# A cross-network kernel: later tail copies for the first group, and tail turns first in the last but one group

## The chip, the cores and the metric

The kernel runs on one NeuronCore of a Trainium2 chip. The metric is device time in microseconds of one execution; most executions of one kernel agree within 0.3%. The profile covers one execution, from its first to its last instruction ("span"); the device time is about 1.8 us longer than that span (498.29 against 496.5 us in the profiled run of the kernel before).

## The reference

Six layers of a "cross network" over 16384 rows of 416 features, in bf16:

```
x = x0                                   # x0: [16384, 416]
for l in range(6):
    proj = x @ ws[l] + bs[l]             # ws[l]: [416, 416]
    x = x0 * proj + x
return x
```

## The kernel before

Rows are handled in 8 groups of 2048. A group is held turned, with features on partitions: three tiles of 128 features ("tiles" t = 0, 1, 2) and a tail of 32 features. A group has four chunks of 512 rows, and the tails of its four chunks are stacked on the four partition quarters. So an output tile is 12 matmuls of full 128 rows, and four of 32 rows that add the tail. ScalarE adds the bias while it empties PSUM, VectorE multiplies by x0 and adds x.

"Turn" in this document means a DMA that transposes. Each group is turned on its way in and out. For the first group, chunks 0 and 1 are loaded plainly and turned by TensorE (quick to start); chunks 2 and 3 are turned by DMA. Before the change, this part of the setup read:

```python
load_nat(0, 0, 2); load_nat(0, 2, KK)      # plain rows of chunk 0   (on SP's queue)
load_wm(0, "sp")                           # weights of layer 0
load_nat(1, 0, KK)                         # plain rows of chunk 1
load_w3(0, "act")                          # four small weight loads, on ScalarE's queue
half = slice(2 * CH, GC)
add("sp", lambda h: h.dma_start_transpose(Tb[:, half], g0[half, D - P:D]), writes=["Tb"], lane="Tb", batch=0)
for t in range(NT):                        # turned tiles of chunks 2 and 3
    add("sp", lambda h, t=t: h.dma_start_transpose(
        x0s[0][:, t * GC + 2 * CH:(t + 1) * GC], g0[half, t * P:(t + 1) * P]), ...)
for j in (2, 3):                           # tail copies, on ScalarE's queue, wait for Tb
    q = slice(j * T32, (j + 1) * T32)
    add("act", lambda h, q=q, j=j: h.dma_start(x0s[0][q, XW:XW + CH], Tb[P - T32:P, j * CH:(j + 1) * CH]),
        reads=["Tb"], writes=[("x03q", 0, j)], ...)
load_wm(1, "sp"); load_w3(1, "sp"); load_group(1)    # load_group(1) turns into Tb again
... (cut)

def first_job():                           # recorded after all of the above
    transposed_chunk(0)                    # TensorE turns; ScalarE and VectorE copy out of PSUM
    ... (bias, cut)
    full(g, l, 0, ba, True, True, chunks=[0])
    transposed_chunk(1)
    full(g, l, 0, ba, True, True, chunks=[1])
    full(g, l, 1, bb, True, True, chunks=[0, 1])
    full(g, l, 0, ba, True, True, chunks=[2, 3])
    rows32(g, l, 0, ba, False)             # first 32-row matmuls
    ... (cut)
```

Every operation goes through `add`, which orders it by its declared tokens: a read waits for the last *recorded* write of its token.

```python
def add(self, eng, fn, reads=(), writes=(), lane=None, batch=None, ...):
    for t in reads:
        w = self.writer.get(t)             # the last recorded writer
        if w is not None:
            deps[id(w)] = (w, True)
    ... (cut)
```

A group goes out through one buffer, `ost`, all on SP's queue, in program order:

```python
def output(g):
    turn(0); turn(1)                       # 128 features each, wait for tile 0 and tile 1
    for j in range(NJ):                    # four turns of the 32-feature tail
        add("sp", ... dma_start_transpose(ost[...], x3s[s3][q, :]) ...)
    turn(2)
    ... one store of ost, 1664 KB (two for group 0), waits for all turns
```

The last group (number 7) is not turned by DMA; TensorE computes its last layer with rows on partitions, and five stores on SP's queue and one on ScalarE's write it. The last output tile before that belongs to group 6: 12 full matmuls, then the four 32-row ones, then two evacuations of 1024 columns.

## Time and profile before

| | before |
|---|---|
| device time, median of 3 | 498.93 us (498.19 to 499.05) |
| span of the profiled run | 496.5 us |
| TensorE busy | 476.4 us |
| TensorE idle in one piece at the head | 5.50 us |
| first 32-row matmuls | 17.9 us |
| store of group 6 issued | 484.17 us |
| that store to the end of the span | 12.3 us |

From the page of the kernel before: the span, TensorE's line of busy time (share of the span, number of instructions), and the chain of waits by engine.

```profile
span 496.5 us, 7997 instructions
...
PE 476.4 (96%) x3205; PEld 200.6 (40%) x3205; DVE 404.0 (81%) x705; ACT 340.8 (69%) x366; POOL 11.6 (2%) x37
...
PE 92%; DVE 2%; DMA 1%; ACT 1%; issue 1%; SPq 0%; ACTq 0%; DVEq 0%
```

TensorE is the limit nearly everywhere, so a gain has to come from the edges. The chain of waits in the first microseconds shows one of them (columns: start in us, duration in us, what the chain stood on; "ACTq" is ScalarE's sequencer issuing a DMA):

```profile
2.67 6.36 DMA Tb<-in_x_dram
...
9.05 0.62 ACTq L494
...
9.69 0.69 ACTq L494
...
10.43 0.61 ACT x L531
...
11.09 1.52 PE ps L418 x3
...
17.93 0.33 PE ps L430 x4
18.25 1.40 PE ps L418 x6
...
27.80 0.61 PE ps L430 x8
```

L494 are the two tail copies; they wait for the turn into `Tb`, issued at 2.67 us, and ScalarE does nothing else until they are issued. L531 are the copies out of PSUM that TensorE waits for. TensorE had turned chunk 0 by 5.3 us, so it sat idle from about 5.6 to 11.09. L430 at 17.93 are the first 32-row matmuls, useful to compare by: all later work hangs on them. (The timelines below give them a start 0.06 to 0.07 us earlier than the chains, 17.86 for 17.93; L430 at 27.80 are those of the second layer.)

The other edge is the end. SP's queue of the kernel before, in order of time (start, duration in us, engine, line, operation, how many):

```profile
468.90 4.50 SPq L597 DMA_TRANSPOSE ost<-x  x2
473.45 6.34 SPq L605 DMA_TRANSPOSE ost<-x  x4
479.83 1.93 SPq L597 DMA_TRANSPOSE ost<-x  x1
484.17 0.37 SPq L615 DMA_DIRECT2D out_dram<-ost  x1
484.58 7.29 SPq L788 DMA_DIRECT2D out_dram<-x  x5
```

Turns 0 and 1 of group 6, its four tail turns, turn 2, then the 1664 KB store (L615), and behind it the stores of the last group (L788). The first two turns waited for VectorE's results; the tail turns, whose data had been ready since 459.7 us, queued behind them. The busy time by stretch (window, its length, busy time of the five engines with instruction counts, granted TensorE clock, busy share of the DMA engines, GB/s) shows what the last 12 us are made of:

```profile
core 0: us, PE busy (x) PEld busy (x) DVE busy (x) ACT busy (x) POOL busy (x), PEclk, DMA share, GB/s
484.20:488.00 3.80, 1.03 (x6) 0.44 (x4) 2.68 (x8) 1.03 (x2) 0.00 (x0) 1.00 0.78 260
488.00:492.00 4.00, 0.00 (x0) 0.00 (x0) 0.00 (x0) 0.00 (x0) 0.00 (x0) 0.63 1.08 339
492.00:496.50 4.50, 0.00 (x0) 0.00 (x0) 0.00 (x0) 0.00 (x0) 0.00 (x0) 0.50 0.79 237
```

From 488 us no engine computes; the DMA engines stream at about 340 GB/s until the last few us.

### The profile page before, as it was taken

What the parts mean: (1) busy time and instruction counts of PE and PEld (TensorE: products, weight loads), DVE (VectorE), ACT (ScalarE), POOL (GpSimd) and SP (SyncE); (2) the same over time, 40 slices, a digit from 0 to 9 for tenths busy, and PEclk for the clock granted to TensorE, in tenths of its full rate; (3) what the DMA queues carried; (4) which work ended last, traced back from release to release, by engine and by line L of the source; (5) the groups of instructions that cost most, each with busy time, mean ns of one, the idle gap of its engine ahead of it and who ended that gap; (6) DMA issues with size and microseconds to landing.
All of it is one profiled execution on the core that took longest, in us unless ns stands there. A gap on an engine that the chain in (4) does not pass through costs nothing.

```text
span 496.5 us, 7997 instructions
## 1 busy us (share of the span) xinstructions
PE 476.4 (96%) x3205; PEld 200.6 (40%) x3205; DVE 404.0 (81%) x705; ACT 340.8 (69%) x366; POOL 11.6 (2%) x37
## 2 busy tenths in 40 slices
PE   4999999999999999999999999999999999999990
PEld 2434434444444444444444444444444444443450
DVE  0578888888888888888888888888888888888892
ACT  2557667677677776677677767766767767776780
POOL 1010400000000000000000000000000000000000
PEclk9999999999999999999999999999999999999997
DMA  9966973000001377449325944460000434316168
GB/s 191 207 137 148 162 166 79 1 0 1 2 0 34 62 206 150 62 85 245 75 39 105 257 56 77 111 228 0 2 1 0 76 64 137 69 27 182 28 113 275
DMA packets 132521, 47.91 MB, mean 97 GB/s; under 512 B 111930, under 2 KB 131588, under 8 KB 132484
## 3 DMA queue, kind: packets, MB, share of 16 engines
q1 hardware_dynamic: 132040, 47.12, 43.0%
q8 instruction: 25, 0.41, 0.3%
q10 hardware_dynamic: 444, 0.28, 0.3%
q14 instruction: 12, 0.10, 0.1%
HBM read 5.12 MB, written 13.63 MB: 38 GB/s over the span
## 4 chain that ended last, share of the span: by engine, by line
PE 92%; DVE 2%; DMA 1%; ACT 1%; issue 1%; SPq 0%; ACTq 0%; DVEq 0%
PE ps L418 74%; PE ps L430 8%; PE ps L443 6%; PE ps L448 2%; PE ps L748 1%; DMA Tb<-in_x_dram 1%; DVE x L391 1%; ACT tw L377 1%; DVE tw L386 1%; PE ps L723 0%; SPq L473 0%; ACTq L494 0%; PE ps L521 0%; PE ps L759 0%; ACT x L776 0%
## 5 line engine op out<-in xcount | busy, mean ns | idle before, releaser
L377 ACT ACTIVATE tw<-ps,bias 128x1024 bf16<-128x1024 f32 (+1 forms) x293 | 299.6, 1076 | 131.5 <-PE ps L430 108.4
L418 PE MATMUL ps<-x,wm 128*128 128x512 bf16 x1692 | 380.4, 380 | 5.9 <-ACT x L531 5.5
L418 PEld LDWEIGHTS ps<-x,wm 128*128 128x128 bf16 x1692 | 159.0, 98 | 220.6 <-issue 28.3
L386 DVE TENSOR_TENSOR tw<-tw,x 128x1024 bf16<-128x1024 bf16 (+1 forms) x283 | 193.2, 687 | 65.8 <-ACT tw L377 65.5
L391 DVE TENSOR_TENSOR x<-tw,x 128x1024 bf16<-128x1024 bf16 (+1 forms) x283 | 181.2, 681 | 0.0
L430 PE MATMUL ps<-x,w 32*128 32x512 bf16 x564 | 44.5, 380 | 0.8 <-DVE x L408 0.8
L443 PE MATMUL ps<-x,wm 128*32 128x512 bf16 x564 | 38.7, 380 | 0.0
L404 ACT ACTIVATE ts<-ps,bias 128x512 bf16<-128x512 f32 x47 | 28.8, 701 | 0.0
L430 PEld LDWEIGHTS ps<-x,w 32*128 32x128 bf16 x564 | 9.1, 92 | 34.1 <-issue 32.6
L443 PEld LDWEIGHTS ps<-x,wm 128*32 128x32 bf16 x564 | 13.8, 96 | 15.7 <-issue 2.9
L408 DVE TENSOR_TENSOR x<-ts,x 128x512 bf16<-128x512 bf16 x47 | 18.6, 418 | 0.0
L406 DVE TENSOR_TENSOR ts<-ts,x 128x512 bf16<-128x512 bf16 x47 | 18.6, 419 | 0.0
L448 PE MATMUL ps<-x,wbd 128*32 128x512 bf16 x188 | 18.3, 379 | 0.0
L534 DVE COPY x<-ps 128x512 bf16<-128x512 bf16 x2 | 0.8, 425 | 12.9 <-PE ps L526 12.9
L293 POOL COPY wbd<-w 32x32 bf16<-32x32 bf16 x24 | 9.5, 396 | 43.2 <-DMA w<-in_ws_dram 42.0
L748 PE MATMUL ps<-wm,x 128*128 128x416 bf16 x48 | 9.2, 341 | 0.0
L531 ACT ACTIVATE x<-ps 128x512 bf16<-128x512 bf16 x4 | 2.2, 594 | 10.1 <-issue 8.2
L776 ACT ACTIVATE x<-ps 128x416 bf16<-128x416 f32 x15 | 7.4, 525 | 1.2 <-PE ps L748 1.1
L448 PEld LDWEIGHTS ps<-x,wbd 128*32 128x32 bf16 x188 | 5.0, 97 | 5.1
L748 PEld LDWEIGHTS ps<-wm,x 128*128 128x128 bf16 x48 | 5.1, 115 | 3.9 <-issue 1.4
L778 DVE TENSOR_TENSOR x<-x,x 128x416 bf16<-128x416 bf16 x15 | 5.5, 371 | 0.5 <-ACT x L776 0.2
L783 DVE TENSOR_TENSOR x<-x,x 128x416 bf16<-128x416 bf16 x16 | 5.6, 368 | 0.0
(36 smaller groups left out, 35.3 us busy)
## 6 DMA issues: line engine op xcount, KB each, us to landing
out_dram<-ost SPq DMA_DIRECT2D x6, 1664.0 KB, 6.9
x<-in_x_dram SPq DMA_DIRECT2D x5, 416.0 KB, 7.5
wm<-in_ws_dram SPq DMA_DIRECT2D x6, 312.0 KB, 3.1
out_dram<-ost SPq DMA_DIRECT2D x2, 832.0 KB, 5.2
out_dram<-x SPq DMA_DIRECT2D x3, 416.0 KB, 7.3
x<-Tb SPq DMA_DIRECT2D x28, 32.0 KB, 1.8
ost<-x SPq DMA_TRANSPOSE x49, 3.4
w<-in_ws_dram SPq DMA_DIRECT2D x20, 26.0 KB, 2.2
```

The lines of the kernel that those rows point to most:

```text
L293: add("pool", lambda h, q=q: h.tensor_copy(wbd[l][q, q], w3[l][q, NT * P:D]), reads=[("w3", l, j)], writes=[("wbd", l)])
L377: add("act", lambda h, a=a, w=w, b0=b0: h.activation(tw[r][:, a * CH:(a + w) * CH], psum[:, b0 * CH:(b0 + w) * CH], ACT_F.Identity, bias=b ...
L386: add("dve", lambda h, a=a, e=e: h.tensor_tensor(tw[r][:, a * CH:e * CH], tw[r][:, a * CH:e * CH], x0s[s0][:, i * GC + a * CH:i * GC + e * ...
L391: add("dve", lambda h, a=a, e=e: h.tensor_tensor(xs[so][:, i * GC + a * CH:i * GC + e * CH], tw[r][:, a * CH:e * CH], src(i, a, e), ALU.ad ...
L404: add("act", lambda h: h.activation(ts[r][:, :], bank(b), ACT_F.Identity, bias=bias[:, 3, l:l + 1], scale=1.0), reads=[("ps", b), "bias"], ...
L406: add("dve", lambda h: h.tensor_tensor(ts[r][:, :], ts[r][:, :], x0s[s0][:, XW:XW + CH], ALU.mult), reads=[("ts", r)] + x03_toks(s0), writ ...
L408: add("dve", lambda h: h.tensor_tensor(x3s[so][:, :], ts[r][:, :], src, ALU.add), reads=[("ts", r)] + stok, writes=[("x3", so)], hold=True)
L418: add("pe", lambda h, t=t, j=j: h.matmul(bank(banks[j]), wm[l][:, t, ecols], src(t, j, j + 1), start=(first and t == 0), stop=(not first a ...
L430: add("pe", lambda h, q=q, j=j: h.matmul(bank(banks[j]), w3[l][q, ecols], src[q, :], start=first, stop=not first, tile_position=(j * T32, 0)),
L443: add("pe", lambda h, t=t, j=j, src=src, l=l, b=b: h.matmul(bank(b, j * T32, (j + 1) * T32), wm[l][:, t, NT * P:D], src(t, j, j + 1), star ...
L448: add("pe", lambda h, j=j, s3=s3, l=l, b=b: h.matmul(bank(b, j * T32, (j + 1) * T32), wbd[l][:, j * T32:(j + 1) * T32], s3, start=False, s ...
L748: add("pe", lambda h, t=t: h.matmul(bank(b, n=D), xcol(t, j, kk), wm[l][:, t, :], start=(first and t == 0), stop=(not first and t == NT - 1)),
```

## The change

Intent: (1) at the head, don't let ScalarE's queue stand on the turned tail; issue the tail copies behind the PSUM copies. For that the tail gets a buffer of its own (a work buffer not used yet), and the four small weight loads go to SP's queue. (2) At the end, let group 6 turn its tails first, and finish its last tile sooner: 32-row matmuls first, then the full ones chunk by chunk, each chunk evacuated on its own.

```diff
-    load_w3(0, "act")
+    load_w3(0, "sp")
@@
-    add("sp", lambda h: h.dma_start_transpose(Tb[:, half], g0[half, D - P:D]), writes=["Tb"], lane="Tb", batch=0)
+    add("sp", lambda h: h.dma_start_transpose(tw[NTW - 1][:, half], g0[half, D - P:D]),
+        writes=[("tw", NTW - 1, j) for j in (2, 3)], lane="Tb0", batch=0)
@@
-    for j in (2, 3):                      # tail copies, in the setup
-        q = slice(j * T32, (j + 1) * T32)
-        add("act", lambda h, q=q, j=j: h.dma_start(x0s[0][q, XW:XW + CH], Tb[P - T32:P, j * CH:(j + 1) * CH]), ...)
@@ first_job
         transposed_chunk(1)
+        for j in (2, 3):
+            q = slice(j * T32, (j + 1) * T32)
+            add("act", lambda h, q=q, j=j: h.dma_start(
+                x0s[0][q, XW:XW + CH], tw[NTW - 1][P - T32:P, j * CH:(j + 1) * CH]),
+                reads=[("tw", NTW - 1, j)], writes=[("x03q", 0, j)], lane="x03_00", batch=0)
@@ output
-        turn(0)
-        turn(1)
+        if g < LAST - 1:
+            turn(0)
+            turn(1)
         ... (four tail turns)
+        if g == LAST - 1:
+            turn(0)
+            turn(1)
         turn(2)
@@ order of matmuls in the last tile
+    mode[len(items) - 1] = "RF"
@@
             rows32(g, l, i, banks, True)
-            full(g, l, i, banks, False, False)
-            evacuate(g, l, i, banks, list(range(NJ)), 2)
+            if n == len(items) - 1:
+                full(g, l, i, banks, False, True, lambda j: evacuate(g, l, i, banks, [j], 1))
+            else:
+                full(g, l, i, banks, False, False)
+                evacuate(g, l, i, banks, list(range(NJ)), 2)
```

More of the change, by code (lines that the diff above doesn't have):

```diff
@@ L491, in bass_standalone__cross_network_dcn__recsys_kernel @@
             writes=[x0_tok(0, t, j) for j in (2, 3)], lane=f"x0_00{t}", batch=0)
-    for j in (2, 3):
-        q = slice(j * T32, (j + 1) * T32)
-        add("act", lambda h, q=q, j=j: h.dma_start(x0s[0][q, XW:XW + CH], Tb[P - T32:P, j * CH:(j + 1) * CH]),
-            reads=["Tb"], writes=[("x03q", 0, j)], lane="x03_00", batch=0)
     load_wm(1, "sp")
```

## The prediction

> **What bounds the kernel.** TensorE: busy 476.4 of 496.5 us (page, part 1), clock granted 0.993; the chain of waits is 92% TensorE. The change touches two stretches outside this middle.
>
> *Head.* The chain stands on a DMA: `Tb<-x0` is issued at 2.67 us and lands at 9.03. ScalarE's queue holds two tail copies that wait for it (9.05, 9.69) ahead of the PSUM copies, so ScalarE starts those at 10.43, although TensorE finished the transposes at 5.3. TensorE sits idle 5.50 us, till 11.09 (view of waits). The first 32-row matmuls follow at 17.93.
>
> *End.* VectorE's last result is at about 487.06, yet the span ends at 496.5. The timeline of SP shows why: for group 6, turns of tiles 0 and 1 from 468.90, four tail turns 473.45 to 479.8, turn 2 at 479.83 (landing 4.3 us later), and only at 484.17 the 1664 KB store, with the last group's five stores behind it. From there the DMA engines move 330 to 350 GB/s to the end: 3.3 MB, 12.3 us. So the end is DMA-bound and starts when turn 2 lands. (The Trainium skill, DMA: Bandwidth & Descriptors, section Bandwidth, gives about 358 GB/s of HBM per core; the trace's 340 agrees, so this stretch can only be started sooner.)
>
> **Change at the head.** The tail copies go behind the second chunk's PSUM copies. ScalarE can copy chunk 0 at about 5; TensorE then waits for the weights (landing 6.6) and the second chunk's rows (7.95), transposes them until about 9.9, and runs nine matmuls until about 12.1. Then a new limit: the three DMA-turned tiles of chunks 2 and 3 (before: landing 10.2, 12.0, 13.3). Moving four weight loads (1.9 us of issue) ahead of them on SP delays them by 0 to 1.9 us; I estimate 13.8 for the last. The tail copies, issued at about 10.3 to 11.5 and taking 4.1 us, land at about 15. So the first 32-row matmuls start near 15.2 instead of 17.93. Estimated gain: 2.7 us, shifting all later work; DMA takes the rest of the idle. Risk: group 1's tails (landing about 29, wanted at 34.0 before, 31.3 after) come late.
>
> **Change at the end.** The tails of group 6 are ready at 459.7 and the previous store lands by about 459, so the four tail turns (6.3 us) run at 460 to 466, while SP is idle. Turns 0 and 1 stay at 468.9 and 471.4, where VectorE's results come. Turn 2 waits for its own tile: with 32-row matmuls first, chunk-major order and four 512-wide evacuations, VectorE ends it at about 474.3 (before 474.77); 4.3 us later, at 478.6, the 1664 KB store goes out instead of at 484.17. The last group's compute (about 0.4 us sooner, ScalarE freeing the banks at about 472.0 instead of 472.83) ends about 486.6, plus 3 to 4 us for the last small store: just inside the stream of stores. Estimated gain: 5.5 us.
>
> **Sum.** 498.93 - 2.7 - 5.5 = 490.7 us; range 488.4 to 494.0. Chances: faster by over 2% (below 488.95) 0.13, within 2% 0.86, slower 0.01.
>
> **Shown right or wrong by:** TensorE's first idle stretch falls from 5.5 us to about 1; the chain's head names x0's turns or the tail copy; first 32-row matmuls near 15.2; tail turns of group 6 near 460; the 1664 KB store near 476 (head shift included); DMA still at about 340 GB/s for the last 10 us.
>
> **What would make it wrong:** x0 turns or tail copies landing over 2 us later than I assume (head gain lost), group 1's loads stalling TensorE near 31 us, or the last group's compute and small stores setting the end.

## The result, and the profile after

The changed kernel takes 490.15 us (median of 4, 489.51 to 491.88); the kernel before took 498.66 us with the runs of the same time added (498.19 to 499.05). The ratio is 0.9835, with a 95% interval of 0.9808 to 0.9862. A ratio here is the mean time of one kernel's runs over the mean of the other's runs of the same rounds, so not quite the ratio of the medians quoted. A second set of five runs gave 490.02 us (489.95 to 490.74), ratio 0.9838, interval 0.9823 to 0.9853.

The page of the changed kernel, the same three lines:

```profile
span 490.1 us, 8003 instructions
...
PE 476.6 (97%) x3205; PEld 199.7 (41%) x3205; DVE 403.7 (82%) x709; ACT 340.6 (69%) x368; POOL 11.5 (2%) x37
...
PE 93%; DVE 2%; SPq 2%; DMA 1%; ACT 1%; issue 0%; DVEq 0%
```

The same TensorE work sits in a span 6.4 us shorter. This profile happens to be of the slowest of the four runs (491.88 us). Its chain of waits at the head:

```profile
9.21 4.90 DMA x<-in_x_dram
...
14.16 1.04 PE ps L418 x4
15.20 0.40 PE ps L430 x4
15.59 2.67 PE ps L418 x6
18.26 0.60 PE ps L430 x4
...
26.63 0.61 PE ps L430 x8
```

The chain no longer stands on the tail but on the last turned tile of chunks 2 and 3, which lands at 14.1 us. The first 32-row matmuls start 2.7 us sooner (15.20 against 17.93). Then something is lost: the six matmuls at 15.59 take 2.67 us, where the kernel before took 1.40 for the same six (18.25 to 19.66 in its chain). The clock by stretch says why:

```profile
14.00:16.00 2.00, 1.84 (x10) 0.62 (x11) 0.35 (x1) 0.39 (x1) 0.00 (x0) 0.83 0.96 233
16.00:18.00 2.00, 2.00 (x6) 0.53 (x4) 2.00 (x5) 0.73 (x1) 1.21 (x5) 0.50 1.03 214
```

TensorE ran at half clock from about 15.3 to 18.7 us. This is not in the second profile of the same kernel (run after_again below); TensorE's timeline there (start, duration, line, operation, with idle time before it in brackets):

```profile
13.97 1.04 PE L418 MATMUL ps<-x,wm 128*128 128x512 bf16 x4 [1.26 <-DMA x<-in_x_dram]
14.95 0.40 PE L430 MATMUL ps<-x,w 32*128 32x512 bf16 x4
15.27 1.47 PE L418 MATMUL ps<-x,wm 128*128 128x512 bf16 x6
```

Its span is 488.3 us instead of 490.1. But the second profile had a slow stretch too, only earlier. The twelve transposes of chunk 1, in the first profile and then in the second:

```profile
7.71 0.84 PE L518 MATMUL ps<-ident,x 128*128 128x128 bf16 x12
...
8.15 1.49 PE L518 MATMUL ps<-ident,x 128*128 128x128 bf16 x12
```

The same work took 1.8 times as long, although both profiles have a clock of 1.00 on record there. It cost little, since TensorE waited afterwards for the turned tile anyway (the 1.26 us above). So the place of a slow stretch decides what it costs, and the clock on record doesn't show this one.

SP's queue at the end of the changed kernel (first profile), to be held against the five lines of before:

```profile
458.53 6.23 SPq L608 DMA_TRANSPOSE ost<-x  x4
467.73 6.51 SPq L599 DMA_TRANSPOSE ost<-x  x3
477.58 0.37 SPq L621 DMA_DIRECT2D out_dram<-ost  x1
478.00 7.75 SPq L798 DMA_DIRECT2D out_dram<-x  x5
```

The tail turns run in a hole that SP had, and the large store goes out at 477.58 instead of 484.17. From there to the end is 12.5 us, against 12.3 before, and the DMA engines stream as before (336 GB/s from 482 to 486 us):

```profile
482.00:486.00 4.00, 1.23 (x7) 0.57 (x5) 2.81 (x9) 1.23 (x3) 0.00 (x0) 1.00 1.09 336
486.00:490.10 4.10, 0.00 (x0) 0.00 (x0) 0.00 (x0) 0.00 (x0) 0.00 (x0) 0.55 0.72 213
```

### The profile page after: what moved, and what is told of

Its sections match the earlier page's. It is cut to its first block, busy times and chain, and to the rows that moved or that the text cites. A ratio compares the mean times of both kernels' runs of the same rounds, so it can differ in the third digit from the quotient of the medians.

```text
span 490.1 us, 8003 instructions
## 1 busy us (share of the span) xinstructions
PE 476.6 (97%) x3205; PEld 199.7 (41%) x3205; DVE 403.7 (82%) x709; ACT 340.6 (69%) x368; POOL 11.5 (2%) x37
## 4 chain that ended last, share of the span: by engine, by line
PE 93%; DVE 2%; SPq 2%; DMA 1%; ACT 1%; issue 0%; DVEq 0%
PE ps L418 74%; PE ps L430 8%; PE ps L443 6%; PE ps L448 2%; PE ps L758 2%; DMA x<-in_x_dram 1%; DVE x L391 1%; DVE tw L386 1%; SPq L490 1%; PE ps L733 1%; ACT tw L377 0%; SPq L286 0%; SPq L473 0%; SPq L487 0%; ACT x L786 0%
## 5 line engine op out<-in xcount | busy, mean ns | idle before, releaser
L443 PEld LDWEIGHTS ps<-x,wm 128*32 128x32 bf16 x564 | 13.8, 96 | 15.7 <-issue 2.9
L361 DVE SCALAR_TENSOR_TENSOR tw<-ps,bias,x 128x512 bf16<-128x512 f32 x2 | 1.4, 746 | 5.9 <-PE ps L430 5.9
L788 DVE TENSOR_TENSOR x<-x,x 128x416 bf16<-128x416 bf16 x15 | 5.5, 371 | 0.4
```

Of the source, the lines that this page charges most:

```text
L443: add("pe", lambda h, t=t, j=j, src=src, l=l, b=b: h.matmul(bank(b, j * T32, (j + 1) * T32), wm[l][:, t, NT * P:D], src(t, j, j + 1), star ...
```

## The experiments

Two landmarks split each profile into three parts: the start of the 32-row matmuls behind the first group's first layer (27.80 us before; all of the head has ended by then), the issue of group 6's store, and the end of the span. In one table (h, i and j change what the landmarks mean and are told below):

| kernel | time, us (median) | ratio to before, same rounds | landmark at | landmark to store | store to end |
|---|---|---|---|---|---|
| before | 498.2 to 498.9 | | 27.80 | 456.4 | 12.3 |
| changed (first profile) | 490.15 | 0.9835 | 26.63 | 451.0 | 12.5 |
| changed (after_again) | 490.02 | 0.9838 | 24.89 | 450.9 | 12.5 |
| a_head_only | 494.97 | 0.9933 | 23.85 | 456.0 | 12.2 |
| b_end_only | 493.75 | 0.9914 | 27.73 | 451.5 | 12.5 |
| c_old_turn_order | 494.84 | 0.9930 | 24.34 | 456.4 | 12.4 |
| d_old_last_tile | 490.56 | 0.9848 | 24.54 | 451.6 | 12.5 |
| e_filler | 489.92 | 0.9835 | 24.73 | 450.9 | 12.6 |
| f_w3_act | 490.24 | 0.9840 | 24.85 | 451.6 | 12.5 |
| g_t_major | 489.37 | 0.9821 | 24.15 | 450.9 | 12.5 |
| k_old_copy_order | 493.38 | 0.9900 | 27.91 | 450.9 | 12.5 |

The intervals of these ratios are 0.0012 to 0.0015 wide on either side, or 0.6 to 0.75 us (0.0027 for the changed kernel's first set). a to d shared one set of rounds, after_again, e, f and g a second, and h to k a third; across sets, ratios are compared.

**a_head_only** is the kernel before with the head's part alone (the pieces of the diff down to `first_job`).

> Only the head's part of the change, the end as in the kernel before. Theory (two independent gains, about 2.7 us at the head and 5.5 at the end, of which the profiled run of the changed kernel lost 1.3 at the head to a stretch of matmuls at half clock): 495.5 to 497.5 us; first 32-row matmuls at about 15.2 us; the 1664 KB store at 481.5 to 483, with the end 12.3 us behind it. Rival (nearly all of the 8.5 us comes from the end, since the head's gain is given back by the half clock or later): within 1.3 us of the kernel before.

Measured: 494.97 us, 0.9933, so 3.3 us gained. The time is just under the expected range. The first 32-row matmuls came at 13.91 us in this profile, with no half clock, because the last turned tile landed at 12.9 us. The head is worth more than expected, and the rival falls.

**b_end_only** is the kernel before with the end's part alone (the pieces in `output` and in the last tile).

> Only the end's two parts (tail turns first, last tile chunk by chunk), the head as before. Theory: about 493.2 us (5.5 us saved), 1664 KB store at about 478.7 us, first 32-row matmuls at 17.9 as before. Rival (the end gives nearly all): about 491.

Measured: 493.75 us, 0.9914, so 4.3 us by the ratio and 4.5 by the medians (498.21 to 493.75). The two halves add up to 7.6 us by their ratios, against 8.1 for both together in the second set; the difference is inside the intervals. The end gives more than the head but less than the 5.5 us expected.

**c_old_turn_order** is the changed kernel with `turn(0); turn(1)` ahead of the tail turns in group 6 again.

> The changed kernel with the old order of turns in the last but one group (turns 0 and 1, four tail turns, turn 2); the last tile still chunk by chunk. Theory: the order of turns is what the end gains, so the 1664 KB store falls back to about 6 us after turn 2 could have gone: about 5.3 us slower than the changed kernel, 495.5 to 497. Rival (the quicker last tile is what frees turn 2): under 1 us slower.

Measured: 494.84 us, 0.9930. Of the end's gain nothing measurable is left: the time is that of a_head_only (494.97, same rounds), although the last tile is still computed in the new way. It is 4.6 us slower than the changed kernel by ratios (4.8 by medians), where 5.3 was expected. SP's queue shows turn 2 standing behind the tail turns again:

```profile
469.90 6.47 SPq L607 DMA_TRANSPOSE ost<-x  x4
476.41 1.39 SPq L599 DMA_TRANSPOSE ost<-x  x1
480.75 0.37 SPq L617 DMA_DIRECT2D out_dram<-ost  x1
```

**d_old_last_tile** is the changed kernel without its last two pieces, so the last tile is computed as before.

```diff
-    mode[len(items) - 1] = "RF"
-            if n == len(items) - 1:
-                full(g, l, i, banks, False, True, lambda j: evacuate(g, l, i, banks, [j], 1))
```

> The changed kernel with the last tile as before (32-row matmuls last, two 1024-wide evacuations), tail turns first. Theory: turn 2 waits for that tile, which is ready 0.4 to 0.5 us later, so 0.3 to 0.6 us slower than the changed kernel. Rival (tile order matters as much as the turns, since TensorE and ScalarE then stall): over 1.5 us slower.

Measured: 490.56 us, 0.9848, against 0.9838 for the changed kernel, so 0.5 us, with intervals that overlap. It is as expected in size, and at the edge of what the rounds can tell. Together, c and d say that the order of the turns carries the end, and the quicker tile adds at most some half a microsecond on top of it.

**after_again** is the changed kernel, unedited.

> The changed kernel again, unedited, for the same rounds as its variants and for a second look at the head. If the half-clock stretch near 15 to 18 us of the first profile is a matter of chance, it may be missing here, and the span of the profiled run is then about 1.3 us shorter for it.

Measured: 490.02 us; no half clock in this profile, and a span of 488.3, 1.8 us shorter than the first one's 490.1. The half clock accounts for 1.27 us of that, the six matmuls alone. Whether the other runs had it can't be seen, since a run without a profile shows only its mean clock.

**e_filler** puts nine idle matmuls where TensorE waits for the turned tiles.

```diff
+        for _ in range(9):
+            add("pe", lambda h: h.matmul(bank(2), ident[:, :], x0s[0][:, 0:CH], start=True, stop=True),
+                reads=["ident", x0_tok(0, 0, 0)], writes=[("ps", 2)])
         full(g, l, 0, ba, True, True, chunks=[2, 3])
```

> The changed kernel with nine idle matmuls (2 us of work, result overwritten) while TensorE waits for the turned tiles of chunks 2 and 3. Theory (TensorE's idle stretch there, about 2.2 us from 11.6 to 14.16, makes the clock drop to half from 15.3 to 18.6 us and costs 1.3 us): no half clock in the head, six matmuls after the first 32-row ones take about 1.4 us instead of 2.74, and the median is 0.3 to 1.3 us lower than the changed kernel's, with less spread. Rival (the half clock is not brought on by this wait, or does not matter as DMA decides later): no difference, or slower by the filler where it outlasts the wait.

Measured: 489.92 us against 490.02 in the same rounds: no difference. No half clock with the filler, but none without it in those rounds' profile either, and none on record in the head of five other variants that kept both the changed order and the wait (a, c, d, f, h). So the loss of the first profile did not come back, and the filler could not be tested against it: what sets it off is not settled. The twelve transposes of chunk 1 fall into two groups as well, all at a recorded clock of 1.00: 0.84 us in the first profile, a, f, h and i, and 1.46 to 1.49 us in after_again, c, d, e, g and j. The Trainium skill, "TensorE: Matmul & The Clock Gate" (Part 1), says that the clock is at half after an idle window of about 3.4 us and at full after a busy one, and that the window runs freely, so that the same kernel meets it differently from run to run. The length agrees: half clock lasted from about 15.3 to 18.7 us, 3.4 us. The start doesn't follow from it: in the 3.40 us before (11.94 to 15.34) TensorE was busy for 1.57 us, so that window was not idle.

**g_t_major** runs the matmuls of chunks 2 and 3 by input tile, for the first two output tiles together, so eight of twelve don't need the last turned tile.

```diff
-        full(g, l, 0, ba, True, True, chunks=[2, 3])
-        rows32(g, l, 0, ba, False)
-        evacuate(g, l, 0, ba, [0, 1], 2, vector=[2, 3])
-        full(g, l, 1, bb, True, True, chunks=[2, 3])
+        for t in range(NT):
+            for i, bks in ((0, ba), (1, bb)):
+                if t == NT - 1 and i == 1:
+                    rows32(g, l, 0, ba, False)
+                    evacuate(g, l, 0, ba, [0, 1], 2, vector=[2, 3])
+                for j in (2, 3):
+                    add("pe", ... matmul(bank(bks[j]), wm[l][:, t, i * P:(i + 1) * P], x0s[0][:, cols(t, j)],
+                                         start=(t == 0), stop=False) ...)
```

> The changed kernel with the matmuls of chunks 2 and 3 of the first two output tiles ordered by input tile, so that eight of twelve run before the last turned tile lands at 14.1 us. Theory (the last turned tile is the head's new limit, then TensorE's work behind it): the eight-matmul block behind the first 32-row ones (18.2 us) starts at about 16 us, a gain of 1 to 2.5 us over the changed kernel. Rival (ScalarE and VectorE evacuation, or the tail copies, is the limit by then): under 0.5 us gained.

Measured: 489.37 us against 490.02, ratio 0.9821 against 0.9838: 0.65 to 0.85 us, between the two expectations. TensorE's timeline shows real work in place of the wait, and then a short new wait, on ScalarE:

```profile
12.19 2.32 PE L572 MATMUL ps<-x,wm 128*128 128x512 bf16 x10
14.45 0.39 PE L430 MATMUL ps<-x,w 32*128 32x512 bf16 x4
14.77 0.60 PE L572 MATMUL ps<-x,wm 128*128 128x512 bf16 x2
15.31 0.40 PE L430 MATMUL ps<-x,w 32*128 32x512 bf16 x4
16.05 0.72 PE L430 MATMUL ps<-x,w 32*128 32x512 bf16 x4 [0.34 <-ACT tw L377]
```

The block of eight 32-row matmuls began at 15.31 instead of 16.67 us in after_again, as the theory said (about 16). At the landmark 0.74 us of these 1.36 are left (24.15 against 24.89). The chain of waits says where the rest went: it now runs from the first 32-row matmuls to VectorE, which empties the other two banks and then multiplies and adds until the landmark, with no TensorE in between:

```profile
14.92 1.40 DVE tw L361 x2
```

So evacuation, the rival's cause, takes about half of it, and on the chain it is VectorE's part.

**f_w3_act** puts the four small weight loads back on ScalarE's queue.

```diff
-    load_w3(0, "sp")
+    load_w3(0, "act")
```

> The changed kernel with the four small weight loads back on ScalarE's queue. Theory (the turned tiles are limited by the DMA engines, which are nearly always busy from 2 to 14 us, not by the 1.9 us of issue on SP): the last turned tile lands within 0.7 us of 14.1, and the time is within 0.7 us. Rival (issue on SP sets the landing): landing near 12.3 and 1.5 us or more faster.

Measured: 490.24 us, 0.9840, no difference; the last turned tile landed at 13.9 us, as in after_again. SP's queue had its 1.9 us back and did nothing with it: the first turn of x0 was issued at 3.98 instead of 5.85 us, but took 3.79 us to issue instead of 2.12, and the third one started at 9.15 instead of 9.36. The Trainium skill, "DMA: Bandwidth & Descriptors" (Issuing engines are not separate DMA queues), says that DMAs of all issuing engines run on the same 16 DMA engines and that a second issuer saves only the time to initiate; this run agrees: for 1.9 us of issue the landing came 0.04 us sooner (13.89 against 13.93 us), less than it varies between profiles of the same head (12.9 to 14.1 us).

**k_old_copy_order** is the changed kernel with the two tail copies recorded where they stood before, ahead of the PSUM copies; own buffer, weight loads and end as changed.

> The changed kernel with the two tail copies back ahead of ScalarE's PSUM copies; own buffer, weight loads on SP and the end as changed. Theory (the order on ScalarE's queue is what the head gains): the head falls back, first 32-row matmuls at 17.5 to 18.5 us, about 3 us slower than the changed kernel, near 493.5. Rival (the moved weight loads or the own buffer carry part of the gain): under 2 us slower.

Measured: 493.38 us, 0.9900 against 0.9838, so 3.1 us lost; the first 32-row matmuls at 17.97 us. ScalarE's timeline has the old picture (9.63 us is when the second copy was issued):

```profile
8.97 1.27 ACTq L495 DMA_DIRECT2D x<-tw  x2
10.28 1.09 ACT L533 ACTIVATE x<-ps 128x512 bf16<-128x512 bf16 x2 [8.05 <-issue]
```

So the gain of the head is the order on ScalarE's queue. What the moved weight loads and the own buffer give without it can't be told from nothing: k and b, which differ in these two alone, have 0.9900 and 0.9914, and their intervals overlap.

**j_shared_buffer** was meant to take away the own buffer only: the first group's tail is turned into `Tb` again, and the copies, in their new place, read `Tb`.

```diff
-    add("sp", lambda h: h.dma_start_transpose(tw[NTW - 1][:, half], g0[half, D - P:D]),
-        writes=[("tw", NTW - 1, j) for j in (2, 3)], lane="Tb0", batch=0)
+    add("sp", lambda h: h.dma_start_transpose(Tb[:, half], g0[half, D - P:D]),
+        writes=["Tb"], lane="Tb", batch=0)
@@
-                x0s[0][q, XW:XW + CH], tw[NTW - 1][P - T32:P, j * CH:(j + 1) * CH]),
-                reads=[("tw", NTW - 1, j)], writes=[("x03q", 0, j)], lane="x03_00", batch=0)
+                x0s[0][q, XW:XW + CH], Tb[P - T32:P, j * CH:(j + 1) * CH]),
+                reads=["Tb"], writes=[("x03q", 0, j)], lane="x03_00", batch=0)
```

> The changed kernel with the tails of the first group turned into the shared buffer as before. Theory (the next turn into that buffer is issued at about 20 us, long after the copies have read it at about 13.8): no difference, within 0.5 us. Rival (the own buffer takes a wait away from SP's queue): 1 us or more slower.

Measured: a wrong result (relative error 0.099) and 504.84 us. The theory missed; the time is in the rival's range, but not for the rival's reason. The fault is in the experiment, in an instructive way. `add` ties a read to the last recorded write. The copies are now recorded after `load_group(1)`, which turns the *second* group's tail into `Tb`; so they waited for that turn and copied the wrong group's tails. ScalarE issued them at 25.11 us, and TensorE stood still:

```profile
28.05 0.61 PE L430 MATMUL ps<-x,w 32*128 32x512 bf16 x4 [13.77 <-DMA x<-Tb]
```

So the own buffer is what lets the copies be recorded later at all. Whether a shared buffer with the right dependences would cost time was therefore not tried. The run still serves as a measure: a wait of 13.77 us at the head, after which TensorE went on at half clock until about 33 us, put the landmark 14.9 us later than in after_again (39.75 against 24.89) and made the kernel 14.8 us slower (504.84 against 490.02), so nothing downstream absorbs a delay there.

**h_kk0_first** moves the last group's first store ahead of group 6's large one.

```diff
+        def store():
+            ... (the 1664 KB store of output(), unchanged)
+        if g == LAST - 1:
+            late.append(store)
+        else:
+            store()
@@
     layer_rows(0, bkb)                    # ends with the last group's first store
+    for f in late:
+        f()
```

> The changed kernel with the first store of the last group (416 KB, ready 1.4 us before turn 2 lands) ahead of the 1664 KB store on SP. Theory (the end is the time of 3.3 MB at about 340 GB/s, counted from the first store): up to 1.2 us saved, but the last results are ready 4.1 us of landing before the end, which caps it: 0.4 to 1.0 us faster. Rival (the end is set by compute and the last small store already): no gain, or the large store and the rest come later and it is slower.

Measured: 489.61 us, 0.9823 against 0.9838, 0.4 us by medians and 0.75 by ratios: as expected, at the edge of the intervals. SP's queue:

```profile
474.03 0.37 SPq L805 DMA_DIRECT2D out_dram<-x  x1
475.48 0.37 SPq L624 DMA_DIRECT2D out_dram<-ost  x1
477.67 5.85 SPq L805 DMA_DIRECT2D out_dram<-x  x4
```

The stream starts 1.45 us before the large store, but the span ends 4.7 us after ScalarE issues the last store at 482.9, of which the landing takes 3.9. That fits the expected cap, the last computed results; but their landing still shares the DMA engines with the rest of the stream, and no run separates the two.

**i_both** combines g and h.

> The changed kernel with both extensions: chunks 2 and 3 by input tile at the head, and the first store of the last group ahead of the large one. Theory: the gains add, 0.65 us at the head and what the store order gave: 488.4 to 489.0 us.

Measured: 488.66 us (487.94 to 488.86), ratio to before 0.9807, interval 0.9794 to 0.9821, correct. That is the fastest kernel, about 1.4 us below the changed kernel by medians (490.02; 1.5 by ratios). It stands right at 2% below the kernel before, so whether it passes that line is unclear.

## Why the prediction was right

The prediction said 490.7 us; measured were 490.15 and 490.02. It named the two waits, and the experiments show that these are where the time went. That the total came so close is partly luck, as the points show:

- *ScalarE's queue stands on the tail copies, and that idles TensorE.* Shown by k: with only their order undone, ScalarE's PSUM copies fall back to 10.28 us and the first 32-row matmuls to 17.97.
- *Only about half of the idle comes back, as the turned tiles of chunks 2 and 3 become the limit.* Shown: the chain stands on them till 14.16 us (estimate 13.8). Their landing differs from profile to profile, from 12.9 (a) to 14.1 us, and with it the time that SP took to issue the first of them (1.29 us in a, 1.98 in the first profile); so the gain at the first 32-row matmuls varies too: 2.7 to 4.0 us.
- *Tail copies landing at about 15 us, so the first 32-row matmuls near 15.2.* The copies were wrong, and the 15.2 that was met (15.20 in the first profile's chain) is luck. The copies were issued at 8.9 and 9.5 us, as the PSUM copies ahead of them began at 8.4 and their own turn had landed by 8.8, and they landed by 13.8, ahead of the last turned tile. What the first 32-row matmuls waited for was that tile (14.1) and then the four full matmuls that come in order from there (1.04 us), which the prediction left out. The moved weight loads were thought to delay the turns by up to 1.9 us; f shows no such delay.
- *Head 2.7 us, shifting all later work.* The size was low: 3.3 (a) and 3.1 (k). In the first profile only 1.2 us of it were left at the landmark (26.63 against 27.80), since matmuls at half clock gave the rest back; the second profile kept 2.9. The prediction did not think of the clock.
- *The end is a stream of 3.3 MB that starts when turn 2 lands.* Shown by the table: store to end is 12.2 to 12.6 us in every listed kernel, while the store itself moves by 5 us.
- *End 5.5 us, by the store going out sooner.* The mechanism was right and the size somewhat high. The store came 5.4 us sooner with respect to the landmark in two profiles of the changed kernel, and 4.9 in b; the time gained 4.3 (b) to 4.7 (after_again against a, by ratios). The term that was too small is the landing of turn 2, 4.6 to 5.3 us after its issue and not 4.3. In a and c, where it followed the tail turns as before, it took 4.3, so what was in flight ahead of it, now turn 1, is the likely reason (not tested apart). The stream was 0.1 to 0.2 us longer besides. In b, d and f the store came 0.6 us later from the landmark than in the others: in d the tile itself was later (turn 2 issued at 471.5 us, 0.7 us later from the landmark than in after_again), while in b and f turn 2 took 1.9 us to issue instead of 1.35 and landed after 5.2 and 5.3 us. Why it has two values stays open.
- *Group 1's tails may come late.* They did not: no wait of TensorE shows near 31 us.
- *Compute stays just inside the stream of stores.* Right and close: h gained less than the 1.4 us by which it started the stream sooner.

The two sizes were off in opposite directions (head too small by 0.4 to 0.6, end too large by 0.8 to 1.2), so the sum of 8.2 us met the measured 8.1 to 8.5 better than its terms did.

## What to carry to other kernels

In these runs a DMA issue that waited held up everything behind it in its engine's queue (ScalarE's copies till 10.28 us in k), so put such an issue behind the work that does not need it, and ask what becomes the limit then, as the wait rarely comes back whole. At the end of a kernel that writes much, find the moment when the last stream of stores can start and pull whatever stands in its queue, but was ready long ago, into an earlier hole. A recorder that orders operations by recorded writes turns a harmless move past a reuse of a buffer into a wrong result; the new buffer is part of such a move.

## What the Trainium skill lacked or had wrong

- "DMA: Bandwidth & Descriptors" gives bandwidths of DMA transposes but no time from issue to landing. Here the 21 turns of 128x2048 within SBUF, in the first profile of the changed kernel, took 1.3 to 3.2 us to issue and landed 4.2 to 6.1 us after their issue began (median 4.4); the 28 turns of a 32x512 tail landed after 2.3 to 7.3 us (median 4.1; 2.4 in the kernel before).
- The same page has nothing on how long an issue by SP can take while earlier transfers are in flight. In f_w3_act an x0 turn took 3.79 us to issue, in after_again, issued 1.9 us later, 2.12 us; both ended at 7.8 to 8.0 us. In a, c and d, issued at the same time as in after_again, it took 1.29, 1.66 and 1.45 us. What sets it is not shown.
- "DMA: Bandwidth & Descriptors" (Where 436 GB/s comes from) gives about 358 GB/s as one core's HBM limit, which the prediction used. But the page's section Bandwidth ties that figure to both cores of a pair streaming, and has 425 GB/s for a 16 MB load by one core alone. It has no measured rate for stores from SBUF on this chip; here the last stores ran at 330 to 345 GB/s (stretches of 2 us), with one core in the program, and no run shows what limits them. So that this stretch "can only be started sooner" is not shown.
- "TensorE: Matmul & The Clock Gate" (Part 1, HAM trace caveats) warns that clock events in traces can't be fully trusted, and it is right: in the kernel before and in b_end_only, with the same code at the head, twelve 128-column transposes took 1.49 us in both, soon after about 5 us of idle, but the clock on record is 1.00 in the first (12 to 14 us) and 0.50 in the second. What the page lacks is a figure for how much work a window must hold to keep the full clock, as in the first profile of the changed kernel (1.57 us of matmuls in the 3.40 us before the half clock); no run here settles it.
